# Seven block products for eight in more of the two channel products of an attention and mixer kernel

## The chip, the cores and the metric

The kernel runs on one core of a Trainium2 chip. The metric is the device time of one execution in microseconds (us). The core's engines work side by side, each through its own list of instructions: PE (TensorE, matmuls; PEld is its weight loads), DVE (VectorE), ACT (ScalarE), POOL (GpSimd, which here only issues the input loads) and SP (SyncE, which issues transposing transfers and stores). An instruction that waits holds up everything behind it on its engine.

## The reference

Shapes: q, k, v are (8 batches, 12 heads, 448 tokens, 64); the two token weights are 448x256 and 256x448, the two channel weights 768x1536 and 1536x768.

```python
scores = scale * np.matmul(q, k.transpose(0, 1, 3, 2))
attn = np.maximum(scores, 0.0) ** 2 / S
x = np.matmul(attn, v)                            # heads side by side: (8, 448, 768)
xt = x.transpose(0, 2, 1)
h = np.maximum(xt @ w_tok1, 0.0) @ w_tok2
u = x + h.transpose(0, 2, 1)
h2 = np.maximum(u @ w_ch1, 0.0) @ w_ch2
return u + h2
```

Attention, then a product over the tokens (the token mixer), then two products over the channels: u times w_ch1 is the first channel product, the ReLU of it times w_ch2 the second.

## The kernel before

All work is cut into named operations (class Op), and a long string, ORDER, lists all of them: every engine walks its own operations in the order of that string, and an operation waits only for those that it depends on. A name in ORDER carries after its colon either the engine (A for ACT, D for DVE) or the PSUM banks that it takes (0 to 7).

Attention runs in 24 groups s of four heads, three groups to a batch. POOL loads k, q and v of a group (ldk, ldq, ldv, two each) into four buffers per kind; a load waits until the group four earlier has let its buffer go. Groups 0 to 9 transpose k and q on PE (T, copies cp); from group 10 on DVE copies them into another layout (ik, iq, L435) and SP issues transposing transfers (xk, xq, L439). For each of seven chunks of keys there are the scores (S, L457: four matmuls on quadrants of the array, with two PSUM banks), their ReLU into bf16 (r, L291 on ACT or L293 on DVE), the square on DVE (q, L467) and the value product (V, L484), which adds up over the chunks in two banks. NSQ = 13 buffers hold squared chunks. The result is evicted to xT (xe, L494 and L496), transposed to x_sb (from group 6 on by a transfer that SP issues, xd, L507), and the token product follows: t1 (L528), its ReLU rt, t2 (L537) and the sum u (L541 on DVE), which is written to uT. A second transposing transfer, ub (L549), brings u into the layout of the output, u_sb.

Two batches make a pair p, with 2 x 448 tokens in seven tiles of 128. The first channel product of a batch (C1, L562) takes for each of 12 blocks of 128 hidden rows six matmuls of 448 columns; c1e (L291, ACT) writes its ReLU to r2. The second (C2, L624) takes for a tile of 128 tokens and each half of the 768 output columns twelve matmuls of 384 columns; c2e (L631, DVE) adds u_sb and writes out_sb, which SP stores (st, L608). uT, u_sb and r2 exist twice, one for the even and one for the odd pairs.

FAST1 and FAST2 name the pairs in which a product is done with seven block products instead of eight: both matrices are cut into 2x2 blocks, sums of blocks are formed ahead of the products, and the products are added to each other afterwards. The weight sums (w1, w2), the sums of u (tu) and of r2 (h) are formed on DVE (L639). In the first product of pair 3 (fast1) the two batches are the two column blocks, so the matmuls have 448 columns (M1, L683); a product that two blocks of the result need is copied out of its bank by ACT (snap, L690), the bank goes on adding the next product, and DVE joins the copy with another bank into r2 (L695); a ReLU on r2 in place follows (z1). In the second product of pairs 2 and 3 (fast2) tiles t and t + 4 are the two row blocks (M2, L748), and DVE adds the products to out_sb one after the other (L759, L761). The middle tile of a pair goes through the plain C2. The block sums of the weights and the copies lie in the arena, the buffers of attention, and in other buffers that are free once attention has ended.

## Time and profile before

| | |
|---|---|
| median of 3 runs | 354.97 us (354.52 to 355.62) |
| the profiled execution | 355.15 us |
| its span, first to last instruction | 353.4 us |
| granted TensorE clock, mean | 0.995 |
| busy ACT, POOL | 193.8 us (55%), 91.8 us (26%) |
| read from and written to HBM | 43.38 MB, 11.01 MB |

The page of the profile gives the busy time of each engine, strips of the span in 40 equal slices (a digit is the busy share in tenths, 9 is 90% or more), the chain of work that ended last, and groups of instructions by line, operation and shape (count, busy us, mean ns of one, then the engine's idle time ahead of them and what ended it). The ends of matmuls are modelled, so two matmuls in a row overlap in the records; the distance from start to start tells what one occupies. DVE's records overlap in the same way: a sum of 448 columns lasts 0.62 us in the records and the next one starts earlier.

### The profile page before, as it was taken

What the parts mean: (1) busy time and instruction counts of PE and PEld (TensorE: products, weight loads), DVE (VectorE), ACT (ScalarE), POOL (GpSimd) and SP (SyncE); (2) the same over time, 40 slices, a digit from 0 to 9 for tenths busy, and PEclk for the clock granted to TensorE, in tenths of its full rate; (3) what the DMA queues carried; (4) which work ended last, traced back from release to release, by engine and by line L of the source; (5) the groups of instructions that cost most, each with busy time, mean ns of one, the idle gap of its engine ahead of it and who ended that gap; (6) DMA issues with size and microseconds to landing.
All of it is one profiled execution on the core that took longest, in us unless ns stands there. A gap on an engine that the chain in (4) does not pass through costs nothing.

```text
span 353.4 us, 8749 instructions
## 1 busy us (share of the span) xinstructions
PE 343.5 (97%) x3489; PEld 191.3 (54%) x3489; DVE 294.8 (83%) x580; ACT 193.8 (55%) x395; POOL 91.8 (26%) x157
## 2 busy tenths in 40 slices
PE   7799999999999999999999999999999999999994
PEld 3456455665555555555555555555545555565663
DVE  3999996878875897989988788978999999995661
ACT  3999996644752666727656565456496165400000
POOL 9886214331460423334403250410000000000000
PEclk9899999999999999999999999999999999999999
DMA  8999999999999989998999899979145220034426
GB/s 151 183 171 163 165 183 206 162 122 155 194 192 130 172 184 156 206 197 158 179 199 140 169 138 176 186 176 184 39 60 92 46 59 2 0 85 141 110 65 183
DMA packets 98297, 50.16 MB, mean 142 GB/s; under 512 B 71440, under 2 KB 94800, under 8 KB 98256
## 3 DMA queue, kind: packets, MB, share of 16 engines
q1 hardware_dynamic: 72880, 27.93, 47.7%
q0 software_dynamic: 25136, 21.47, 46.4%
q8 instruction: 27, 0.44, 0.5%
q10 hardware_dynamic: 240, 0.20, 0.2%
q14 instruction: 14, 0.11, 0.1%
HBM read 43.38 MB, written 11.01 MB: 154 GB/s over the span
## 4 chain that ended last, share of the span: by engine, by line
PE 91%; DVE 5%; DMA 1%; ACT 0%; issue 0%; SPq 0%
PE m_ps L562 24%; PE m_ps L624 18%; PE m_ps L748 12%; PE sc_ps L457 10%; PE acc_ps L484 9%; PE m_ps L683 7%; PE t_ps L528 6%; PE h_ps L537 5%; DVE arena L467 2%; DMA arena<-in_q_dram 1%; PE kqT_ps L414 1%; DVE uT_sb L541 1%; DVE arena L639 1%; PE x_ps L519 1%; DVE arena L293 1%; DVE arena L299 1%
## 5 line engine op out<-in xcount | busy, mean ns | idle before, releaser
L291 ACT ACTIVATE arena<-sc_ps 128x448 bf16<-128x448 f32 x234 | 112.0, 573 | 28.8 <-PE sc_ps L457 27.6
L467 DVE TENSOR_TENSOR arena<-arena 128x896 bf16<-128x896 bf16 x168 | 97.0, 618 | 0.5
L562 PE MATMUL m_ps<-uT_sb,wc 128*128 128x448 bf16 x432 | 89.5, 353 | 0.6 <-DVE uT_sb L541 0.6
L293 DVE TENSOR_SCALAR arena<-sc_ps 128x448 bf16<-128x448 f32 x102 | 59.5, 617 | 9.7 <-PE sc_ps L457 9.6
L624 PE MATMUL m_ps<-wc,r_sb 128*128 128x384 bf16 (+2 forms) x396 | 66.6, 322 | 0.0
L562 PEld LDWEIGHTS <-wc 128*128 128x128 bf16 x432 | 40.2, 98 | 43.1 <-issue 9.2
L291 ACT ACTIVATE r_sb<-m_ps 128x448 bf16<-128x448 f32 x72 | 39.7, 553 | 42.4 <-PE m_ps L562 41.9
L313 POOL DMA_DIRECT2D arena<-in_v_dram x48 | 29.3, 620 | 118.3 <-PE sc_ps L457 75.2
L457 PE MATMUL sc_ps<-arena 64*64 64x448 bf16 x672 | 54.4, 361 | 0.7 <-DVE arena L299 0.2
L624 PEld LDWEIGHTS <-r_sb 128*128 128x128 bf16 x396 | 37.7, 98 | 26.3 <-issue 2.6
L484 PE MATMUL acc_ps<-arena 64*64 64x448 bf16 x672 | 49.2, 358 | 1.8 <-DVE arena L467 1.8
L541 DVE TENSOR_TENSOR uT_sb<-h_ps,xT 128x448 bf16<-128x448 f32 x48 | 28.6, 618 | 5.9 <-PE h_ps L537 5.8
L313 POOL DMA_DIRECT2D arena<-in_k_dram x48 | 29.6, 629 | 14.8 <-DMA wc<-in_moe_w_ch_dram 6.5
L457 PEld LDWEIGHTS <-arena 64*64 64x64 bf16 x672 | 20.5, 107 | 20.7 <-issue 12.6
L313 POOL DMA_DIRECT2D arena<-in_q_dram x46 | 28.7, 639 | 9.3 <-PE sc_ps L457 4.7
L484 PEld LDWEIGHTS <-arena 64*64 64x64 bf16 x672 | 20.8, 108 | 15.5 <-issue 6.8
L631 DVE TENSOR_TENSOR out_sb<-m_ps,u_sb 128x384 f32<-128x384 f32 (+2 forms) x31 | 16.8, 543 | 14.3 <-PE m_ps L624 14.1
L291 ACT ACTIVATE r_sb<-t_ps 128x512 bf16<-128x512 f32 (+1 forms) x26 | 15.0, 585 | 20.1 <-PE t_ps L528 20.0
L528 PE MATMUL t_ps<-x_sb,wt 128*128 128x256 bf16 (+1 forms) x216 | 25.4, 261 | 0.0
L537 PE MATMUL h_ps<-wt,r_sb 128*128 128x448 bf16 x96 | 23.8, 354 | 0.0
L528 PEld LDWEIGHTS <-wt 128*128 128x128 bf16 x216 | 19.0, 98 | 7.1 <-issue 1.8
L435 DVE COPY arena<-arena 128x896 bf16<-128x896 bf16 x28 | 16.9, 612 | 4.3 <-DMA arena<-in_q_dram 2.9
(67 smaller groups left out, 300.1 us busy)
## 6 DMA issues: line engine op xcount, KB each, us to landing
out_dram<-out_sb SPq DMA_DIRECT2D x46, 192.0 KB, 3.9
arena<-in_k_dram POOLq DMA_DIRECT2D x48, 112.0 KB, 6.0
arena<-in_v_dram POOLq DMA_DIRECT2D x48, 112.0 KB, 5.3
arena<-in_q_dram POOLq DMA_DIRECT2D x46, 112.0 KB, 7.4
wc<-in_moe_w_ch_dram POOLq DMA_DIRECT2D x6, 768.0 KB, 18.5
out_dram<-xT SPq DMA_DIRECT2D x8, 192.0 KB, 2.8
u_sb<-uT_sb SPq DMA_TRANSPOSE x48, 5.0
arena<-in_q_dram SPq DMA_DIRECT2D x2, 224.0 KB, 3.9
```

The source lines that it names most:

```text
L291: nc.scalar.activation(out, ps, AF.Relu)
L293: nc.vector.tensor_scalar(out=out, in0=ps, scalar1=0.0, scalar2=None, op0=ALU.max)
L313: nc.gpsimd.dma_start(out=raws[t][s % NR][64 * half:64 * (half + 1)], in_=src[b, h0:h0 + 2].rearrange('e (p c) d -> p e (c d)', c=KC))
L457: nc.tensor.matmul(o.ps[e][64 * half:64 * (half + 1), :S], lhsT=lhsT, rhs=rhs, start=True, stop=True, skip_group_check=True)
L467: sq_ops[s, c] = [add(Op(f'q{s}.{c}', 'DVE', lambda o: nc.vector.tensor_tensor(out=buf, in0=buf, in1=buf, op=ALU.mult), ev))]
L484: nc.tensor.matmul(o.ps[half][64 * e:64 * (e + 1), :S], lhsT=r[rows, e, c * D:(c + 1) * D], rhs=sq[rows, e, :], start=c == 0, stop=c == KC ...
L528: nc.tensor.matmul(o.ps[:, j, :], lhsT=wt1[:, c, j * 128:(j + 1) * 128], rhs=x_sb[:, p0:p1, c, :], start=c == 0, stop=c == 3)
L537: nc.tensor.matmul(o.ps[:, :S], lhsT=r1[:, j, a * 128:(a + 1) * 128], rhs=wt2[:, j, :], start=j == 0, stop=j == JC - 1)
L541: nc.vector.tensor_tensor(out=uTs[bb % 2][:, 2 * i + a, off:off + S].rearrange('n (c p) -> n c p', c=KC), in0=t2.ps[:, :S].rearrange('n (p ...
L562: nc.tensor.matmul(ps[:, :S], lhsT=wc1[:, g, e * 128:(e + 1) * 128], rhs=uT[:, g, off:off + S], start=g == 0, stop=g == CC - 1)
L624: nc.tensor.matmul(o.ps[:, :size], lhsT=r2[:, e, t * 128:(t + 1) * 128], rhs=wc2[:, e, cols], start=e == 0, stop=e == EC - 1)
L748: nc.tensor.matmul(o.ps[:, :HN], lhsT=lhs[:, e], rhs=rhs[:, e], start=e == 0 and not on, stop=e == EC // 2 - 1, skip_group_check=True)
```

## The change

The first product is done with seven products in every batch from 2 on (FIRST1), each batch by itself: its 448 tokens are cut into two halves of 224, and a product does two blocks of hidden rows (e, e + 1) in the two halves of one PSUM bank, each with three matmuls of 224 columns. m1, m6, m7 and m4 add up in one bank, m5 and m3 in another. Snapshots are kept as fp32 in rows of r2 that are written later. The second product is done with seven products for three pairs of tiles in all four pairs of batches; PAIRS names them. The tile that is left (ALONE) goes through C2, which now multiplies its upper half with the sum of both halves of r2, since one block of wc2 has been replaced in place by a difference.

r2 and u_sb exist once for pairs 0 to 2 (pair 3 takes the arena), uT has room for three batches, which neighbouring pairs share, the weight sums have a buffer of their own, there are 12 buffers for squared chunks instead of 13 and four output buffers instead of three (two more in the arena at the end). ORDER is replaced from group 5 of attention on; the entries ahead of that are the same. By count of its entries: 27 C1 and 9 C2 (before 75 and 33), 126 M1 and 84 M2 (42 and 42), 54 snapshots (18), 54 joins (24), 84 sums into out_sb behind M2 (48), 52 sums of r2 (48), 24 sums of u (4), 36 z1 and 18 y1 (12 z1); of the score copies r, 284 on ACT and 52 on DVE (234 and 102).

```diff
 NSIDE = 2
 SPLIT = 1
 FUSED = set()
-FAST1, FAST2 = ({3}, {2, 3})
-TILES = [*range(14), 14, 18, 15, 19, 16, 20, 17, 21, 25, 22, 26, 23, 27, 24]
+FIRST1 = 2
+PAIRS = {0: [(0, 1), (3, 4), (5, 6)], 1: [(4, 5), (0, 1), (2, 3)]}
+PAIRS[2], PAIRS[3] = PAIRS[0], [(5, 6), (0, 1), (2, 3)]
+ALONE = [2, 6, 2, 4]
+TILES = [7 * p + t for p, order in enumerate(((0, 1, 2, 3, 4, 5, 6), (4, 5, 6, 0, 1, 2, 3), (0, 1, 2, 3, 4, 5, 6), (5, 6, 0, 1, 2, 3, 4))) for t in order]
+
 
 class Op:
 
...
-r15.2.1:D V14.5 V14.6 r15.6.0:A S16.4:14 r15.6.1:D ldv18.0 C2.1.0.1:7 xe14.0:A xe14.1:D r16.4.0:A ldv18.1
-q15.1:D r16.4.1:A xd14 ldk19.0 q15.2:D ldk19.1 q15.5:D S16.3:26 S16.5:53 ldq19.0 S16.2:01 r16.3.0:A c2e1.0.1:D
...
+r15.0.1:A V14.4 u13.1:D V14.5 V14.6 ldq19.0 S16.0:65 tu3.1:D M1.3.0.1:1 r16.0.1:A q15.0:D ldv16.0 r16.0.0:A
+M2.1.4.4 q15.3:D ldq20.1 s1.3.0.1:A xe14.1:A M1.3.0.3 d2.1.4.21:D xe14.0:A tu3.3:D S15.5:75 S15.6:63 S16.1:42
+r15.5.0:A q16.0:D xq18 M1.3.0.6 r16.1.1:A r15.5.1:D r15.6.1:A M1.3.0.2:7 q15.2:D r16.1.0:A C2.1.6.1:2 xq17
+d1.3.0.11:D q15.1:D s1.3.0.2:A q15.5:D r15.6.0:A xd14 d1.3.0.12:D M1.3.0.7 q15.4:D S16.4:53 V15.0:47 xk18
...
-    NR, NQ, NSQ, NX, NO = (4, 3, 13, 3, 3)
+    NR, NQ, NSQ, NX, NO = (4, 3, 12, 3, 4)
...
-    uTs = [sbuf.tile([128, CC, 2 * S], BF16, name=f'uT_sb{i}') for i in range(2)]
-    u_sbs = [sbuf.tile([128, CC, NT, 128], BF16, name=f'u_sb{i}') for i in range(2)]
-    r2s = [sbuf.tile([128, EC, 2 * S], BF16, name=f'r2_sb{i}') for i in range(2)]
+    uT_all = sbuf.tile([128, CC, 3 * S], BF16, name='uT')
+    uT2 = [uT_all[:, :, p % 2 * S:p % 2 * S + 2 * S] for p in range(B // 2)]
+    u_sb = sbuf.tile([128, CC, NT, 128], BF16, name='u_sb')
+    r2 = sbuf.tile([128, EC, 2 * S], BF16, name='r2')
...
+    u_sbs = [u_sb] * 3 + [arena[:, late['u'][0]:late['u'][1]].rearrange('p (g t n) -> p g t n', g=CC, t=NT)]
+    r2s = [r2] * 3 + [piece(late['r2'][0], EC * 2 * S, EC)]
...
+    def side(b):
+
+        return (b % 2 ^ b // 2 % 2) * S
+
+    def whole(p, b):
+
+        return range(3) if p % 2 == 0 and b == 0 else range(3, NT) if p % 2 == 0 else range(4, NT) if b == 0 else range(4)
+
+    def uslot(p, t):
+        return t if p % 2 == 0 else (t + 3) % NT
...
+    def tokens(p, t):
+
+        got = []
+        for b in (2 * p, 2 * p + 1):
+            if side(b) < (t + 1) * 128 and t * 128 < side(b) + S:
+                for e in range(EC):
+                    got += c1e[b, e]
+        return got
+
+    def u_part(p, t, g0, g1):
+        b = [b for b in range(2) if t in whole(p, b)][0]
+        return (u_sbs[p][:, g0:g1, uslot(p, t), :], [ub[2 * p + b, g] for g in range(g0, g1)])
+
+    def add2(name, dst, x, y, op, deps, **kw):
+        return add(Op(name, 'DVE', lambda o: nc.vector.tensor_tensor(out=dst, in0=x, in1=y, op=op), deps, **kw))
+
+    def sum_set(p):
+        k = sum_n[p == 3] % (1 if p < 3 else 3)
+        sum_n[p == 3] += 1
+        return (rsum[k], sum_free[k])
...
+        rows = tokens(bb, t)
+        (both, _, _), free = sum_set(bb)
+        h = add2(f'h{bb}.{t}.s', both, r2[:, :EC // 2, at], r2[:, EC // 2:, at], ALU.add, rows + free[0])
+        free[0] = []
...
+                    x = both[:, e - EC // 2] if high and e >= EC // 2 else r2[:, e, at]
+                    nc.tensor.matmul(o.ps[:, :size], lhsT=x, rhs=wc2[:, e, cols], start=e == 0, stop=e == EC - 1)
...
             if k == 2:
                 x = one(0, dst[0], w12, w11, ALU.subtract, [])
+                one(3, w12, w12, w22, ALU.subtract, x)
                 y = one(1, dst[1], w22, dst[0], ALU.subtract, x)
-                one(2, dst[2], w22, w12, ALU.subtract, [])
-                one(3, dst[3], dst[1], w21, ALU.subtract, y)
+                one(2, dst[2], w21, dst[1], ALU.subtract, y)
             else:
                 x = one(0, dst[0], w21, w22, ALU.add, [])
...
+    def fast1(b):
+        p = b // 2
+        r2, off = (r2s[p], side(b))
+        uT = uT2[p][:, :, off:off + S]
+        first = b % 2 == 0 and p % 2 == 0
+        half = [slice(HB, S), slice(0, HB)] if first else [slice(0, HB), slice(HB, S)]
+        u11, u12, u21, u22 = (uT[:, g:g + 3, c] for g in (0, 3) for c in half)
+        parts = [[ue[s, a] for a in range(2)] for s in range(GS * b, GS * (b + 1))]
+        low, high = (parts[0] + parts[1][:1], parts[1][1:] + parts[2])
+        every = low + high
+        tu, free = ([u12, *tu_own], [] if b == FIRST1 else reads1[b - 1]) if b < 7 else (tu_late, users(*late['tu']))
+        t3_ = add2(f'tu{b}.2', tu[2], u22, u12, ALU.subtract, every + free)
+        t1_ = add2(f'tu{b}.0', tu[0], u12, u11, ALU.subtract, low + [t3_] + [ub[b, g] for g in range(3)] if b < 7 else low + free)
+        t2_ = add2(f'tu{b}.1', tu[1], u22, tu[0], ALU.subtract, [t1_] + high + free + (snap_free[0] if b < 7 else []))
+        t4_ = add2(f'tu{b}.3', tu[3], u21, tu[1], ALU.subtract, [t2_] + high + free)
+        free2 = [o for t in range(NT) if p and off < (t + 1) * 128 and t * 128 < off + S for o in reads2[p - 1, t]] if p < 3 else users(*late['r2'])
+        reads1[b] = []
+        got, spare = ({}, {})
+        for e in range(0, EC // 2, 2):
+
+            def product(name, lhs, rhs, deps, on=None):
+                o = Op(f'M1.{b}.{e}.{name}', 'PE', None, deps, banks=0 if on else 1, holder=on)
+
+                def emit(o, e=e):
+                    for j in range(2):
+                        for g in range(3):
+                            nc.tensor.matmul(o.ps[:, j * HB:(j + 1) * HB], lhsT=lhs[:, g, (e + j) * 128:(e + j + 1) * 128], rhs=rhs[:, g], start=j == g == 0 and not on, stop=g == 2, skip_group_check=True)
+                reads1[b].append(o)
+                got[e, name] = add(o)
+                return o
+
+            def block(hi, c):
+                return r2[:, hi * 6 + e:hi * 6 + e + 2, off + half[c].start:off + half[c].stop]
+
+            def two(u):
+                return u.ps[:, :S].rearrange('p (j n) -> p j n', j=2)
+
+            def snap(name, dst, u, deps):
+                return add(Op(f's1.{b}.{e}.{name}', 'ACT', lambda o: nc.scalar.activation(dst, two(u), AF.Copy), [u, *deps], reads=[u]))
+
+            def join(name, dst, x, u, deps):
+                o = add(Op(f'd1.{b}.{e}.{name}', 'DVE', lambda o: nc.vector.tensor_tensor(out=dst, in0=x, in1=two(u), op=ALU.add), [u, *deps], reads=[u]))
+                got[e, 'd' + name] = o
+                return o
+
+            def fp32(row):
+                return r2[:, row:row + 2, off:off + S].bitcast(FP32)
+            A = lambda i, h: wc1[:, 3 * i:3 * i + 3, h * DC // 2:(h + 1) * DC // 2]
+            inside = fp32(6 + e)
+            before1 = free2 + ([got[2, 'd22']] if e == 4 else [])
+            m1 = product('1', A(0, 0), u11, every + ([got[e - 2, '5']] if e else []))
+            m2 = product('2', A(1, 0), u21, every)
+            a1 = snap('1', inside, m1, before1)
+            c11 = join('11', block(0, 0), inside, m2, [a1] + ([got[0, 'd22']] if e == 4 else []))
+            m6 = product('6', ws1[1], tu[1], [t2_, a1] + ws_ops[1, 1], m1)
+            a2 = snap('2', inside, m6, [c11])
+            m5 = product('5', ws1[0], tu[0], [t1_] + ws_ops[1, 0])
+            if e == 4:
+                k = 0 if b < 6 else 1 + b % 2
+                x, deps = (snaps[k], [got[i, '6'] for i in (0, 2, 4)] if b < 6 else snap_free[k])
+            else:
+                x, deps = (fp32(4 if e == 0 else 10), free2)
+            a5 = snap('5', x, m5, deps)
+            m3 = product('3', ws1[2], u22, every + [a5] + ws_ops[1, 3], m5)
+            c12 = join('12', block(0, 1), inside, m3, [a2])
+            za = add(Op(f'z1.{b}.{e}.a', 'DVE', lambda o, e=e: relu(o, r2[:, e:e + 2, off:off + S], r2[:, e:e + 2, off:off + S]), [c11, c12]))
+            m7 = product('7', A(0, 1), tu[2], [t3_, a2] + ws_ops[1, 2], m1)
+            c22 = join('22', block(1, 1), x, m7, [a5, c12])
+            if e == 4:
+                snap_free[k] = [c22]
+            zc = add(Op(f'z1.{b}.{e}.c', 'DVE', lambda o, d=block(1, 1): relu(o, d, d), [c22]))
+            m4 = product('4', A(1, 1), tu[3], [t4_, c22], m1)
+            y = add(Op(f'y1.{b}.{e}', 'ACT', lambda o, d=block(1, 0), m4=m4: relu(o, d, two(m4)), [m4, c12], reads=[m4]))
+            for j in range(2):
+                c1e[b, e + j] = [za]
+                c1e[b, 6 + e + j] = [zc, y]
+
...
+    def fast2(p, t, q):
+        r2 = r2s[p]
+        (s1, s2, s4), free = sum_set(p)
+        out1, parts, store1 = stores(p, t)
...
+        x = add2(f'h{p}.{t}.0', s1, h21, h22, ALU.add, co + free[0])
+        y = add2(f'h{p}.{t}.1', s2, s1, h11, ALU.subtract, [x] + ce + free[1])
+        w = add2(f'h{p}.{t}.2', h21, h21, h11, ALU.subtract, [x] + ce)
+        z = add2(f'h{p}.{t}.3', s4, h12, s2, ALU.subtract, [y] + free[2])
+        w2 = list(wc2_ops.values())
+        m2 = product('2', r2[:, e_hi, te], wc2[:, e_hi, c_lo], ce + w2)
+        m1 = product('1', r2[:, e_lo, te], wc2[:, e_lo, c_lo], ce + w2)
+        f11 = take('11a', t, c_lo, m2, [], True)
+        g11 = take('11b', t, c_lo, m1, [f11], False)
+        m6 = product('6', s2, ws2[1], [y, g11] + ws_ops[2, 1], m1)
+        f12 = take('12a', t, c_hi, m6, [], True)
+        m5 = product('5', s1, ws2[0], [x] + ws_ops[2, 0])
+        f22 = take('22a', q, c_hi, m5, [], True)
+        m3 = product('3', s4, wc2[:, e_hi, c_hi], [z, f22] + w2, m5)
+        g12 = take('12b', t, c_hi, m3, [f12], False)
+        m7 = product('7', r2[:, e_lo, to], wc2[:, e_lo, c_hi], [w, f12] + ws_ops[2, 3], m1)
+        g22 = take('22b', q, c_hi, m7, [f22], False)
+        m4 = product('4', r2[:, e_hi, to], ws2[2], co + [g22] + ws_ops[2, 2], m1)
+        g21 = take('21', q, c_lo, m4, [], True)
+        free[:] = [[m5, y], [m6, z], [m3]]
+        for n, s_, ends in ((t, store1, [g11, g12]), (q, store2, [g21, g22])):
+            s_(f'{p * NT + n}', slice(0, DM), ends)
...
+            if b == FIRST1:
...
+            if b < FIRST1:
+                for e in range(EC):
                     channel1(b, e, b == 0 and e < PARTIAL)
+            else:
+                fast1(b)
+            if p < 3:
+                done = [t for t in range(NT) if t in whole(p, b % 2)]
+                todo = [x for x in PAIRS[p] if x[0] in done]
+                first, then = (todo, [ALONE[p]] if ALONE[p] in done else [])
+            else:
+                first, then = ([x for x in PAIRS[p] if x[0] in whole(p, b % 2)], [ALONE[p]] if b % 2 else [])
+            for x, y in first:
+                fast2(p, x, y)
+            for x in then:
```

546 lines of the change are left out of this document (249 added, 297 removed).

## The prediction

> **What bounds the kernel now.** I read the page first: the busy sums, then the strips of 40 slices.
>
> ```profile
> span 353.4 us, 8749 instructions
> ...
> PE 343.5 (97%) x3489; PEld 191.3 (54%) x3489; DVE 294.8 (83%) x580; ACT 193.8 (55%) x395; POOL 91.8 (26%) x157
> ...
> PE   7799999999999999999999999999999999999994
> ...
> DVE  3999996878875897989988788978999999995661
> ```
>
> TensorE (PE) is busy for 97% of the span. VectorE (DVE) is second with 83%, and its strip shows nines beside the sevens: averages hide where it binds. So I asked for the busy time in five stretches (columns: stretch, length, busy PE, PEld, DVE, ACT, POOL, clock, DMA share, GB/s).
>
> ```profile
> 34.70:118.50 83.80, 83.80 (x1038) 46.80 (x1036) 67.96 (x126) 54.22 (x111) 26.83 (x45) 1.00 1.36 170
> 118.50:251.50 133.00, 133.00 (x1222) 72.89 (x1221) 114.33 (x212) 79.43 (x167) 36.20 (x61) 1.00 1.12 168
> 251.50:301.40 49.90, 49.30 (x367) 25.57 (x365) 49.90 (x110) 27.98 (x53) 0.00 (x0) 1.00 0.30 53
> 301.40:332.50 31.10, 31.10 (x191) 18.48 (x189) 24.86 (x58) 3.80 (x4) 0.00 (x0) 1.00 0.33 88
> 332.50:353.40 20.90, 15.84 (x110) 10.05 (x107) 9.75 (x19) 0.00 (x0) 0.00 (x0) 0.99 0.42 115
> ```
>
> PE has no idle time from 34.7 to 251.5 us, with DVE at 81 to 86%. From 251.5 to 301.4 DVE is busy for 49.90 of 49.90 us: that stretch holds the weight sums, the sums for the last first product and the end of attention. From 301.4 on PE alone binds. A modelled end can make a waiting PE look busy, so the chain of waits is the test:
>
> ```profile
> 279.52 21.10 PE m_ps L683 x111
> ...
> 307.36 37.05 PE m_ps L748 x228
> ```
>
> Both products that already use seven blocks for eight (L683 and L748) run as unbroken PE work: 21.10 us for 111 matmuls is 0.190 us each at 448 columns, 37.05 us for 228 is 0.1625 us each at 384 columns. PE is at its streaming rate where no attention runs, although L683 hands a bank to ACT or DVE between products. Less streaming is therefore worth nearly its whole price, as long as DVE keeps up.
>
> **The change on PE.** What one matmul occupies is read from start to start in the order of time (start, length, what, count):
>
> ```profile
> 27.34 0.61 PE L528 MATMUL t_ps<-x_sb,wt 128*128 128x128 bf16 x8
> 27.79 0.39 PE L519 MATMUL x_ps<-ident,xT 128*128 128x128 bf16 x4
> ...
> 99.67 1.87 PE L562 MATMUL m_ps<-uT_sb,wc 128*128 128x448 bf16 x9
> 101.37 1.04 PE L528 MATMUL t_ps<-x_sb,wt 128*128 128x256 bf16 x8
> 102.24 0.92 PE L537 MATMUL h_ps<-wt,r_sb 128*128 128x448 bf16 x4
> ```
>
> 128 columns: (27.79 - 27.34)/8 = 0.056 us. 448 columns: (101.37 - 99.67)/9 = 0.189. 256 columns: (102.24 - 101.37)/8 = 0.109. The new narrow matmuls have 224 columns and no row of their own; on the line between 128 and 256 they cost 0.056 + 96/128 x 0.053 = 0.0957 us. The ends are half a 448 (0.0945) and a full 256 (0.109). I take 0.0957, since 128 to 448 lie on one line.
>
> ```profile
> L562 PE MATMUL m_ps<-uT_sb,wc 128*128 128x448 bf16 x432 | 89.5, 353 | 0.6 <-DVE uT_sb L541 0.6
> L624 PE MATMUL m_ps<-wc,r_sb 128*128 128x384 bf16 x372 | 64.6, 327 | 0.0
> ...
> L528 PEld LDWEIGHTS <-wt 128*128 128x128 bf16 x216 | 19.0, 98 | 7.1 <-issue 1.8 <-DMA arena<-in_q_dram 0.4 <-DMA x_sb<-xT 0.4
> ```
>
> First product: now 432 matmuls of 448 (L562, batches 0 to 5) and 126 at L683 (3 each in 42 products): 558 x 0.189 = 105.5 us. After: 12 x 6 = 72 for each of batches 0 and 1, 144 x 0.189 = 27.2; for each of six batches 3 row pairs x 7 products x 6 = 126 narrow ones, 756 x 0.0957 = 72.3. Sum 99.5: **-6.0 us**, all of it from batches 2 to 5 (6 and 7 go from 23.8 to 24.1). At the ends -6.9 and +4.0.
>
> Second product: now 372 of 384 columns, 12 more in the split last tile, and 252 at L748, 636 in all. After: twelve pairs of tiles x 42 and four single tiles x 24 = 600. 36 x 0.1625 = **-5.9 us**. PE together: **-11.9 us**.
>
> The row of weight loads at L528 speaks to the narrow price: one load for each matmul, 98 ns long each, and still the eight matmuls of 128 columns above start 56 ns apart, so the loads overlap. The Trainium skill ("TensorE: Matmul & The Clock Gate", section "LDWEIGHTS (loading the stationary operand)") states columns/1.2 ns for a load, 107 ns here; if loads followed each other at that price, 756 x (0.107 - 0.0957) = 8.5 us would come back, an estimate from that page. The 56 ns disagree with it as a floor.
>
> **The change on DVE.** Again from start to start:
>
> ```profile
> 166.74 2.75 DVE L467 TENSOR_TENSOR arena<-arena 128x896 bf16<-128x896 bf16 x5
> 169.41 0.55 DVE L631 TENSOR_TENSOR out_sb<-m_ps,u_sb 128x384 f32<-128x384 f32 x1
> ...
> 270.99 1.43 DVE L639 TENSOR_TENSOR arena<-r_sb 128x384 bf16<-128x384 bf16 x5
> 272.34 0.35 DVE L639 TENSOR_TENSOR arena<-arena,r_sb 128x384 bf16<-128x384 bf16 x1
> 272.61 1.49 DVE L639 TENSOR_TENSOR arena<-wc 128x768 bf16<-128x768 bf16 x3
> 274.01 1.49 DVE L639 TENSOR_TENSOR arena<-arena,wc 128x768 bf16<-128x768 bf16 x3
> ...
> 288.34 0.70 DVE L293 TENSOR_SCALAR r_sb<-r_sb 128x896 bf16<-128x896 bf16 x2
> 288.94 0.62 DVE L695 TENSOR_TENSOR r_sb<-x_sb,m_ps 128x448 bf16<-128x448 f32 x1
> ...
> 293.52 0.62 DVE L695 TENSOR_TENSOR r_sb<-r_sb,m_ps 128x448 bf16<-128x448 f32 x1
> 294.05 0.63 DVE L639 TENSOR_TENSOR arena<-r_sb,arena 128x384 bf16<-128x384 bf16 x2
> ...
> 302.87 0.56 DVE L761 TENSOR_TENSOR out_sb<-out_sb,m_ps 128x384 f32<-128x384 f32 x1
> 303.33 0.64 DVE L639 TENSOR_TENSOR arena<-arena,r_sb 128x384 bf16<-128x384 bf16 x2
> ```
>
> Square or PSUM copy of 448 columns (x5): (169.41 - 166.74)/5 = 0.534 us. bf16 sum of 384: 0.27; of 768: (274.01 - 272.61)/3 = 0.467. In-place ReLU of 896: 0.30. Join of a snapshot with a bank: 0.53. Output sum of 384: 0.46.
>
> Counts are from the two written orders. Added: joins 24 to 54, +30 x 0.53 = 15.9. Output sums 81 to 93, 12 x 0.47 = 5.6. Sums of hidden rows, from 48 of 384 elements (12.9) to 52 of 768 (24.3), +11.4. Input sums, from 4 of 1344 (3.1, extrapolated) to 24 of 672 (0.42 by the line, 10.1), +7.0. ReLUs, from 5 of 896 to 18 of 896 and 18 of 448 (between 0 and 0.30, taken 0.19), +7.4. Four ReLUs of y1, five of c1e and two rt that move from ACT, +6. Removed: score copies on DVE 102 to 52, -26.7, and attention evictions 24 to 16, -4.3. Sum **+22 us**: DVE's own work rises from 287 to about 310 us, just above PE's 305. ACT goes from 175 to 191 and has room. The twenty weight sums cost what they did, 11 us, but leave the stretch at 250 to 282 where DVE bound and go into batches 0 and 1.
>
> DVE work costs time only where it exceeds PE's in the same piece of the order. I cut each order into ten stretches of equal PE work, priced every entry as above (S and V at 0.187 for four quadrants together, about one pass of 448) and took the largest engine in each:
>
> before 43.3, 32.0, 31.1, 31.8, 31.6, 31.8, 32.4, 33.5, 31.8, 31.2: 330.4, of which PE 316.8;
> after 41.2, 32.2, 31.7, 32.2, 31.5, 31.7, 30.4, 31.1, 30.2, 30.3: 322.5, of which PE 304.9.
>
> DVE is the larger one in stretches 2 to 6 of after and in the eighth. The surplus over PE goes from 13.6 to 17.6: **+4.0 us** of the gain is given back. With 40 stretches it is +6.8, with 60 +1.8; these are the ends. The 23 us between 330.4 and the span (the first load, the last store, a few tenths at each handover) I leave as they are.
>
> **Transfers.** Counts stay (48 ub, 18 xd, 28 crossings, 60 stores, the same loads). SP and POOL are walked in order, so what counts is the cover: the PE work listed between a transfer and its user. Loads of k gain cover (7.9 to 36 us of DVE work to the crossing copy, before 3.7 to 13); those of v range wider (5.3 to 59 us of PE work, before 9 to 47). One u_sb and one r2 in place of two make ub wait for the outputs of the pair before; the shortest covers are 5.2 to 6.3 us for four of 48, free at the end. The xd transposes (xT to x_sb, before each token product t1) lose cover: in the loaded phase eight have 4.1 to 6.3 us, where before none had under 9.0. While t1 waits, PE's whole queue waits behind it. Now:
>
> ```profile
>   PEld L528: 0.4, 1
> ```
>
> PE's token product waited once. Landing of xd, min/median/max, first in 70 to 235 us, then in 235 to 285 us, where no loads run:
>
> ```profile
> DMA to landing us min/median/max: 4.8/7.8/13.1
> ```
>
> ```profile
> DMA to landing us min/median/max: 3.1/3.6/4.4
> ```
>
> All in time is 0. All eight late at the loaded median is 8 x 7.8 - 1.1 x 42.8 us of summed cover (1.1 is span over priced PE work) = +15.3. The order decides between them: before, a V that frees a v buffer is followed by six loads right ahead of nearly every xd; after, seven of the eight short ones (groups 6, 8, 12, 13, 14, 16, 19) have no load released in the 3 us ahead of them, only up to four behind. They should land near 3.6. Group 7 has seven loads around it. I take **+1.0**.
>
> **Tail.** The last DVE sum now ends at 348.67, 4.7 us before the span does, ahead of a store of 32 KB.
>
> ```profile
> 348.38 0.29 DVE L631 TENSOR_TENSOR out_sb<-m_ps,u_sb 128x128 f32<-128x128 f32 x1 [0.24 <-PE m_ps L624]
> ```
>
> ```profile
> DMA to landing us min/median/max: 1.8/2.8/4.1
> ```
>
> (Landing of the stores after 340 us.) After, two stores of 192 KB follow the last sum on one queue: about 1.0 more to land (2.8 for 1.8) and one more issue: **+1.5**, between 0 and 3.
>
> **Sum.** -11.9 + 4.0 + 1.0 + 1.5 = -5.4 us: span 353.4 - 5.4 = 348.0. The profiled execution took 355.15, 1.75 around the span: 349.7. It stood 0.2 above the median of the runs (354.97): **349.5 us**. Its own range, from the ends of the DVE and tail terms, is 346 to 353.
>
> **Rivals.**
> PE alone binds. DVE's surplus is absorbed as in the 251.5 to 301.4 stretch, where DVE ran without a gap, so stretches even out: -11.9 + 1.5 = -10.4, 344.6 us. For it: PE loses nothing after 301.4. Against: there DVE had twenty weight sums that nobody waited for at once.
> Late transposes, the slower side. Place: t1 of groups 6 to 19. Price: up to 15.3, and with five of eight late 9.6, which gives 349.5 - 1.0 + 9.6 = 358.1. It decides from 6.4 us in all, 0.8 for each of the eight. For it: the 7.8; against: the 3.6 without loads.
> Handover chains. Each row pair passes one bank through m1, snapshot, m6, snapshot and join, m7, m4; with DVE full, each hop waits in its queue. 18 pairs x 0.3 us = 5.4: 354.9, no change. For it: DVE's nines; against: the unbroken 21.10 us at L683.
> Narrow products gain nothing: 0.109 each, as 256 columns, +10.1: 359.6. Against: 56 ns at 128 columns. (The 107 ns that the Trainium skill's page above states for a weight load would end in the same place, 358.0, by its estimate.) That the products aren't cut at all is excluded by the counts in the order (126 M1, 84 M2).
>
> **How the numbers follow.** Forecast 0.52, PE alone 0.17, late transposes 0.18, chains 0.10, narrow 0.03. A measurement of this kernel tells about 0.3% (1.1 us) from no change. Faster takes nearly all of the first two and a third of the chains: 0.71; same 0.08 (chains, a mild case of late transposes); slower 0.21. The range reaches down past PE alone with less lost at the tail, 343, and up to the late transposes' 358.
>
> **What would show it.** 756 matmuls of 224 columns 0.096 us apart (not 0.107); 504 + 96 of the second product; PE busy near 331 us; DVE busy 94 to 96% from 35 to 270 us; waits of the token product for x_sb under 2 us in total; weight sums between 45 and 90 us; no DVE-bound stretch at the end. It is wrong if PE waits for x_sb or for joins by more than 6 us, or if the span is set by DVE gaps rather than PE's.

## The result, and the profile after

The changed kernel took 352.83 us (median of 20 runs, 350.96 to 356.98), the kernel before 355.29 us beside it (20 runs, 354.08 to 360.06): a ratio of 0.9934, 95% interval 0.9909 to 0.9959. It is faster by 0.7%, some 2.3 us, where 5.4 us were forecast. A second set gave 353.5 us (11 runs) and 0.9952 (0.9919 to 0.9984). The ratios leave out the longest runs as disturbed; where this document gives means, they hold all runs, because what lengthens them is part of the question, and without the longest ones too the mean granted clock is 0.9953 before and 0.9904 after.

The page of the changed kernel's first profiled execution (it took 356.81 us, the next to longest of the 20):

```profile
span 355.0 us, 9385 instructions
...
PE 338.9 (95%) x3795; PEld 218.7 (62%) x3795; DVE 316.1 (89%) x630; ACT 209.2 (59%) x441; POOL 92.0 (26%) x157
...
PE   7799999999999799999969999999999999999993
...
PEclk9999999999999989999996999999999999999999
```

and of another execution of the same kernel, in experiment e1:

```profile
span 350.2 us, 9385 instructions
...
PE 335.4 (96%) x3795; PEld 217.2 (62%) x3795; DVE 316.0 (90%) x630; ACT 209.5 (60%) x441; POOL 91.8 (26%) x157
...
PE   8799999999998979979999999999999999999993
...
PEclk9999999999999999999999999999999999999998
```

One program, 4.8 us apart. PE now shows sevens and sixes in the middle, where before had only nines, and in the longer execution the granted clock dips in the slices right behind them (an 8 and a 6). So I read the spans of e1's execution for the work and the waits, and the first one for what the clock adds. The kernel before had 53 runs beside the experiments; with the changed kernel's 31 the means are 355.86 and 353.60 us, 2.3 us apart.

The busy time of e1's execution in the stretches that the prediction showed for before (columns as there; the last row runs from 35 to 270 us):

```profile
34.70:118.50 83.80, 82.60 (x1023) 44.40 (x1020) 79.96 (x151) 56.97 (x117) 25.66 (x43) 1.00 1.11 163
118.50:251.50 133.00, 128.98 (x1368) 85.42 (x1367) 126.10 (x254) 99.63 (x215) 37.36 (x63) 1.00 1.08 164
251.50:301.40 49.90, 49.90 (x495) 38.08 (x494) 47.58 (x96) 17.95 (x36) 0.00 (x0) 1.00 0.35 66
301.40:332.50 31.10, 31.10 (x266) 24.98 (x264) 24.35 (x53) 5.84 (x12) 0.00 (x0) 1.00 0.50 99
332.50:350.20 17.70, 12.13 (x75) 7.08 (x73) 9.29 (x19) 0.00 (x0) 0.00 (x0) 0.93 0.49 123
35.00:270.00 235.00, 229.78 (x2573) 144.27 (x2567) 223.71 (x440) 163.46 (x345) 62.88 (x106) 1.00 1.05 159
```

From 34.7 to 251.5 us PE used to have no idle time at all; now 5.2 us are missing (83.80 - 82.60 + 133.00 - 128.98). DVE is at 95% of that time. The stretch from 251.5 us, where DVE used to be busy without a gap, has PE without a gap instead.

Where the time went shows when both spans are cut into the prediction's ten stretches of equal PE work, whose larger engine it priced at 330.4 us in all before and at 322.5 after. The span takes 23.0 us more than that sum before, 27.7 in e1's execution: if PE and DVE together brought the -7.9 of the sum, +4.7 stand behind it. The 4.7 lie in the third to the fifth stretch. First before, then e1:

```profile
86.40:118.50 32.10, 32.10 (x272) 17.66 (x271) 24.20 (x45) 18.48 (x38) 11.26 (x19) 1.00 1.38 172
118.50:151.80 33.30, 33.30 (x312) 17.78 (x311) 28.86 (x55) 21.15 (x45) 12.47 (x22) 1.00 1.19 179
151.80:184.70 32.90, 32.90 (x313) 18.16 (x315) 29.67 (x56) 19.14 (x41) 8.31 (x15) 1.00 1.19 178
```

```profile
83.10:117.40 34.30, 33.23 (x310) 17.14 (x299) 32.16 (x63) 23.85 (x52) 5.37 (x10) 1.00 1.16 167
117.40:152.40 35.00, 32.93 (x356) 22.57 (x354) 32.51 (x66) 25.48 (x56) 13.06 (x22) 1.00 1.13 158
152.40:186.90 34.50, 32.55 (x343) 20.36 (x341) 31.78 (x63) 25.77 (x56) 14.50 (x25) 1.00 1.16 180
```

They took 98.3 us before and 103.8 after. The priced work of the larger engine went from 94.5 to 95.4 us (31.1, 31.8, 31.6 and 31.7, 32.2, 31.5), so time beyond it went from 3.8 to 8.4 us: +4.6. The other seven stretches together moved by 0.1 us. (Before's profile has a stretch of halved clock at 15 to 18 us and e1's has none: in the same order of work the first row of ten matmuls of 448 columns starts at 39.27 us before and at 38.64 in e1, so the 0.1 holds to some 0.6.) In these three stretches DVE is the larger engine by price, 95.4 us; it was busy for 96.5 and idle for 7.4, of which 5.8 are the waits for u_sb below.

The waits of e1's execution (who, for what; us in all, times, longest), PE's first, then DVE's:

```profile
PE t_ps L574 <- DMA x_sb<-xT: 2.3, 2, 2.0
...
PE m_ps L833 <- DVE out_sb L846: 1.5, 1, 1.5
```

```profile
DVE uT L672 <- DMA u_sb<-uT: 3.8, 2, 2.1
...
DVE out_sb L846 <- DMA u_sb<-uT: 2.0, 1, 2.0
```

The first is the token product t1 (L574) waiting for its transpose xd, of which the prediction had spoken. The second is PE waiting for DVE, and the DVE rows say why: DVE waits for u_sb, the transposing copies ub. Neither DVE row exists before. `DVE uT L672` is tu{b}.0, the first sum of a batch's input columns. It is written in place over a block of uT that the copies ub still have to read.

The first profile shows such a chain, and what follows it. In the order of time (start, length, what, and in brackets the idle time before it):

```profile
123.51 0.51 DVE L672 TENSOR_TENSOR uT<-uT 128x672 bf16<-128x672 bf16 x1 [3.13 <-DMA u_sb<-uT]
123.93 0.55 DVE L846 TENSOR_TENSOR out_sb<-u_sb,m_ps 128x384 f32<-128x384 bf16 x1
...
124.53 1.85 PE L833 MATMUL m_ps<-wc,r 128*128 128x384 bf16 x6 [2.06 <-DVE out_sb L846]
```

DVE stands at tu2.0 for 3.13 us; behind it in its queue is the sum that empties a bank (L846); the second product waits 2.06 us for that bank. Then its six matmuls take 1.85 us, where six of 384 columns took 1.14 elsewhere. The clock says why (the same view in stretches cut where the granted clock changes, then the same around a wait of 3.65 us of t1.14 for x_sb that ended at 187.0):

```profile
121.40:124.80 3.40, 1.34 (x16) 0.70 (x14) 1.29 (x3) 1.91 (x4) 3.28 (x7) 1.00 0.95 137
124.80:128.20 3.40, 3.40 (x30) 1.50 (x31) 3.40 (x8) 1.06 (x3) 3.40 (x7) 0.50 1.26 199
...
182.00:186.20 4.20, 1.39 (x15) 1.14 (x12) 1.41 (x3) 2.37 (x6) 3.42 (x6) 1.00 1.54 146
186.20:193.10 6.90, 6.06 (x33) 3.63 (x34) 3.50 (x8) 2.29 (x5) 0.00 (x0) 0.51 1.18 204
```

After a stretch in which PE is busy for about a third, it runs at half its clock for 3.4 or 6.8 us: up to half of that, 1.7 and 3.4 us, is lost on top of the wait. The halved stretch begins 2.3 us after the wait did in the first case (124.53 - 2.06 = 122.47, then 124.8), 2.8 us after in the second. Over the 20 runs the time follows the mean clock: 351.48 us at 0.995, 356.98 us at 0.981.

### The profile page after: what moved, and what is told of

Read it like the earlier page. It is cut to its first block, busy times and chain, and to the rows that moved or that the text cites. A ratio compares the mean times of both kernels' runs of the same rounds, so it can differ in the third digit from the quotient of the medians.

```text
span 355.0 us, 9385 instructions
## 1 busy us (share of the span) xinstructions
PE 338.9 (95%) x3795; PEld 218.7 (62%) x3795; DVE 316.1 (89%) x630; ACT 209.2 (59%) x441; POOL 92.0 (26%) x157
## 4 chain that ended last, share of the span: by engine, by line
PE 82%; DMA 7%; DVE 7%; ACT 1%; issue 1%; POOL 0%; SPq 0%; DVEq 0%; POOLq 0%; ACTq 0%
PE m_ps L764 21%; PE m_ps L833 20%; PE sc_ps L503 9%; PE acc_ps L530 8%; PE m_ps L609 8%; PE t_ps L574 6%; PE h_ps L583 5%; PE m_ps L697 4%; DMA x_sb<-xT 2%; DVE arena L513 2%; DMA u_sb<-uT 2%; DMA arena<-in_k_dram 1%; DMA out_dram<-out_sb 1%; PE kqT_ps L460 1%; ACT arena L337 1%
## 5 line engine op out<-in xcount | busy, mean ns | idle before, releaser
L337 ACT ACTIVATE arena<-sc_ps 128x448 bf16<-128x448 f32 x284 | 137.1, 568 | 34.8 <-PE sc_ps L503 30.5
L764 PEld LDWEIGHTS <-wc 128*128 128x128 bf16 x432 | 40.8, 98 | 6.7 <-issue 3.9
L764 PEld LDWEIGHTS <-ws 128*128 128x128 bf16 x324 | 31.1, 100 | 4.9 <-issue 3.0
L339 DVE TENSOR_SCALAR arena<-sc_ps 128x448 bf16<-128x448 f32 x52 | 31.4, 620 | 1.7 <-PE sc_ps L503 1.6
L833 PE MATMUL m_ps<-wc,r 128*128 128x384 bf16 x162 | 30.9, 332 | 2.1 <-DVE out_sb L846 2.1
L833 PEld LDWEIGHTS <-r 128*128 128x128 bf16 x216 | 20.6, 98 | 17.4 <-issue 5.2
L609 PE MATMUL m_ps<-uT,wc 128*128 128x448 bf16 x144 | 30.0, 353 | 0.0
L574 PE MATMUL t_ps<-x_sb,wt 128*128 128x256 bf16 (+1 forms) x216 | 26.2, 266 | 3.6 <-DMA x_sb<-xT 3.6
L587 DVE TENSOR_TENSOR uT<-h_ps,xT 128x448 bf16<-128x448 f32 x48 | 29.1, 622 | 0.5 <-PE h_ps L583 0.4
L777 ACT ACTIVATE arena<-m_ps 128x448 f32<-128x448 f32 x18 | 9.5, 545 | 32.7 <-PE m_ps L764 23.3
L777 ACT ACTIVATE r<-m_ps 128x448 f32<-128x448 f32 x32 | 17.5, 554 | 16.0 <-PE m_ps L764 10.7
L764 PE MATMUL m_ps<-uT,wc 128*128 128x224 bf16 x216 | 25.7, 259 | 0.0
L574 PEld LDWEIGHTS <-wt 128*128 128x128 bf16 x216 | 19.4, 99 | 9.4 <-DMA x_sb<-xT 3.9
```

The lines of the kernel that those rows point to most:

```text
L337: nc.scalar.activation(out, ps, AF.Relu)
L339: nc.vector.tensor_scalar(out=out, in0=ps, scalar1=0.0, scalar2=None, op0=ALU.max)
L574: nc.tensor.matmul(o.ps[:, j, :], lhsT=wt1[:, c, j * 128:(j + 1) * 128], rhs=x_sb[:, p0:p1, c, :], start=c == 0, stop=c == 3)
L587: nc.vector.tensor_tensor(out=uT2[bb][:, 2 * i + a, off:off + S].rearrange('n (c p) -> n c p', c=KC), in0=t2.ps[:, :S].rearrange('n (p c) ...
L609: nc.tensor.matmul(ps[:, :S], lhsT=wc1[:, g, e * 128:(e + 1) * 128], rhs=uT[:, g, off:off + S], start=g == 0, stop=g == CC - 1)
L764: nc.tensor.matmul(o.ps[:, j * HB:(j + 1) * HB], lhsT=lhs[:, g, (e + j) * 128:(e + j + 1) * 128], rhs=rhs[:, g], start=j == g == 0 and not ...
```

## The experiments

Two main theories. **A**: the gain was given back at a few waits for transfers (t1 for xd, tu2.0 and the output sums for ub), each followed by more loss through the clock. **B**: DVE's surplus over PE costs more than the 4.0 us priced. **C**, in some of the expectations: the clock falls by itself, or by a disturbance of the chip, and not after waits. Runs of one kind are put together in this table. "Clock" is the mean granted clock over the span; "by the clock" is span x (1 - clock), what full speed would have saved if PE worked all of the slow time, so an upper bound (e1's profiled execution is halved only from 347.5 us on, when PE has no work left, and still has 1.05 us in this column); "rest" is the time without it. All are means.

| kernel | runs | time us | clock | by the clock | rest |
|---|---|---|---|---|---|
| before | 53 | 355.86 | 0.9953 | 1.68 | 354.18 |
| after (with e1) | 31 | 353.60 | 0.9895 | 3.68 | 349.92 |
| e2: xd14 earlier | 12 | 355.83 | 0.9868 | 4.67 | 351.16 |
| e3 and e10: tu2.0 later | 12 | 352.45 | 0.9949 | 1.79 | 350.66 |
| e4: both | 8 | 352.89 | 0.9925 | 2.64 | 350.25 |
| e5: e3 without ReLUs | 4 | 352.12 | 0.9892 | 3.78 | 348.34 |
| e8 and e11: more cover | 19 | 352.28 | 0.9923 | 2.70 | 349.58 |
| e6: before, xd14 late | 4 | 364.37 | 0.9862 | 4.99 | 359.39 |
| e9: before, xd14 half as late | 4 | 364.00 | 0.9842 | 5.70 | 358.30 |
| e7: e6 with PE kept busy | 4 | 364.19 | 0.9970 | 1.09 | 363.10 |

**e1, the changed kernel again.** No edit.

> The changed kernel once more, for a profile and a ratio beside the variants. Theory A (two transfers come late and PE pays for each twice, once by waiting and once by a halved clock afterwards): the gain over the kernel before is about 2.5 us, ratio 0.993, mean granted clock 0.988 to 0.993 where the kernel before has 0.995, and the waits show PE held for x_sb in front of the token product of group 14 (around 183 us) and DVE held by a transfer out of uT (around 120 us). Theory B (VectorE's surplus work is the loss): no such waits, clock 0.995, DVE above 96% from 35 to 270 us. Theory C (the clock falls by itself, from more power): clock falls at places without a PE wait.

353.5 us (11 runs), ratio 0.9952 (0.9919 to 0.9984). Its profile is the one read above. Against the first profile the waits differ in place and length (the longest for x_sb is 2.0 us here, 3.65 there): which transfer comes late changes from execution to execution.

**e2, one transpose earlier; e3, one sum later; e4, both.** In the written order:

```
e2   d2.1.4.21:D xe14.0:A  + xd14  tu3.3:D
     ...
     r15.6.0:A  - xd14  d1.3.0.12:D
e3   ldv11.0 d2.0.3.12b:D M2.0.5.3  - tu2.0:D  ldq17.0
     ...
     r11.6.1:A d2.0.3.22b:D  + tu2.0:D  V10.5
```

> Only the transfer xd14 is listed earlier on SP, right behind the eviction xe14.0 and so ahead of the crossing transfers xq18 and xq17, which wait for the scores of group 15. Theory A: the transfer is issued about 3 us earlier, PE's wait of 3.7 us in front of t1.14 goes, the clock stays up there, and the time falls by 2 to 5 us against e1 (ratio to the kernel before 0.980 to 0.988). Theory B: no change beyond 0.3%. A rival within A (the landing is slow because of the loads around it, not because of SP's queue): it is issued earlier but still lands at the same time, and nothing changes.

> Only the sum tu2.0, which overwrites part of uT and so waits for the transfer ub2.0 out of it, is listed nine DVE operations later (about 4.5 us). Theory A: DVE's wait of 3.1 us around 120 us goes, with it PE's wait of 2 us behind it, and the time falls by 1 to 3 us against e1. Theory B: no change beyond 0.3%.

> Both moves. Theory A: the gains add up, 3 to 7 us against e1, span 345 to 348 us, clock 0.994 or more, ratio to the kernel before 0.975 to 0.984. Theory B: as e1. Theory C: the clock stays at 0.990 and the time at e1's.

e2 alone gains nothing where 2 to 5 us were expected: median 356.58 us (12 runs), ratio 0.9931 (0.9887 to 0.9975). In its profile t1.14 no longer waits, but the u_sb wait and one for a store are there, and PE waits longer than ever for DVE:

```profile
PE m_ps L833 <- DVE out_sb L846: 6.0, 2, 4.0
...
DVE uT L672 <- DMA u_sb<-uT: 4.6, 1, 4.6
...
DVE out_sb L846 <- DMA out_dram<-out_sb: 2.9, 1, 2.9
```

e3 took 351.06 us (6 runs), ratio 0.985 (0.9811 to 0.989), with a profile of 348.6 us: DVE's wait at L672 for u_sb is gone, 1.3 us for x_sb, 1.7 for u_sb at an output sum and 2.7 for a store remain. e4 gave 352.31 us (8 runs), ratio 0.9869 (0.9822 to 0.9916), and none of these waits in its profile of 349.1 us, which was halved in its clock twice before 20 us; its gain on e1 is 1.2 us by the medians and not the 3 to 7 expected, so the two moves don't add up. These four kernels ran in the same rounds: moving tu2.0 lowers the mean by 2.9 us both without and with e2's move (354.27 to 351.33, 355.83 to 352.89; standard errors 1.1 and 1.3), and e2's move raises it by 1.6 both times, within the noise. So the wait at tu2.0 looks like one cause, and e2's place isn't shown to be one.

**e10, e3 once more.**

> e3_tu2_late a second time. Theory A: again 350 to 352 us, mean clock 0.993 or over. If its six runs were luck, 352 to 353.5 us as the changed kernel, and a mean clock near 0.989.

353.95 us (6 runs, 348.79 to 357.05), ratio 0.9882 (0.9824 to 0.9941), above the 350 to 352 that A expected: with it, the mean of the twelve is 352.45 us, and about half of e3's advantage over the changed kernel (351.33 to 353.60) is gone. Its profile (span 352.9) shows another transfer late, a store of 192 KB from a tile out_sb, with eight loads of POOL issued around it:

```profile
208.95 0.55 DVE L846 TENSOR_TENSOR out_sb<-u_sb,m_ps 128x384 f32<-128x384 bf16 x1 [4.07 <-DMA out_dram<-out_sb]
...
209.56 1.76 PE L833 MATMUL m_ps<-wc,sums 128*128 128x384 bf16 x5 [3.68 <-DVE out_sb L846]
```

```profile
190.00:205.80 15.80, 15.80 (x176) 9.85 (x169) 14.40 (x29) 12.28 (x27) 4.68 (x9) 1.00 1.05 188
205.80:208.20 2.40, 0.07 (x1) 0.00 (x0) 0.00 (x0) 0.00 (x0) 0.66 (x2) 1.00 1.78 85
208.20:215.00 6.80, 5.45 (x25) 2.08 (x25) 3.93 (x8) 0.48 (x2) 1.78 (x3) 0.50 1.40 121
```

For 2.4 us hardly an engine but POOL works; then the clock is halved for 6.8 us. It is the same chain with another transfer at its head.

**e5, less work for DVE.** e3's kernel without the 36 ReLUs in place of the first and third kind:

```
-    za = add(Op(..., lambda o, e=e: relu(o, r2[:, e:e + 2, off:off + S], ...), [c11, c12]))
+    za = add(Op(..., lambda o: None, [c11, c12]))
-    zc = add(Op(..., lambda o, d=block(1, 1): relu(o, d, d), [c22]))
+    zc = add(Op(..., lambda o: None, [c22]))
```

> The kernel of e3_tu2_late with the 36 in-place ReLUs of the hidden rows (first and third kind, batches 2 to 7) left out, so those hidden rows are computed without ReLU: 18 of 896 columns at 0.30 us and 18 of 448 at about 0.19 us, 8.8 us of VectorE's work. Theory A (the gain was given back at a few waits for transfers, and the surplus of VectorE's work over TensorE's is the 4 us that the prediction priced): the most it can return is that surplus, so 0 to 4 us below e3_tu2_late, and the waits for x_sb and u_sb stay. Theory B (VectorE's work is what keeps the time up): it returns nearly all of its work, 6 to 9 us below e3_tu2_late, about 343 to 345 us.

352.02 us (4 runs), beside 352.0 (the median of e3's and e10's twelve); DVE was busy for 309.0 us in place of 315.5. Nowhere near 343 to 345 though DVE had 6.5 us less to do: B falls as the main cause. The rest without the clock is 2.3 us lower (348.34 for 350.66), within A's 0 to 4, but on four runs. One execution again waited 2.0 us for x_sb and ran at half its clock from 158.6 to 162.0 us.

**e6, e9, e7, the price of one wait.** The kernel before, where no such wait existed, with the entry of the transpose for group 14 moved down: in e6 to right in front of t1.14, in e9 some 2.2 us of PE work ahead of it, in e7 as e6 with 28 matmuls of 512 columns between (27 of them recorded).

```
     r16.4.1:A  - xd14  ldk19.0
     ...
e9   iq19:D  + xd14  S17.0:76
e6   r17.1.1:A q17.0:D  + xd14  t1.14.0:6
e7   r17.1.1:A q17.0:D  + xd14 fill:6*112  t1.14.0:6
```

> The kernel before with one entry of its order moved: the transpose of x for group 14 is listed right in front of the token product that reads it. Theory A: TensorE waits once for its landing, 3 to 8 us, and then runs at half its clock for one or two stretches of 3.4 us, which costs 1.7 or 3.4 us more: 4 to 11 us above the kernel before, and more than the wait alone by 1.7 us or over. A rival, C (a wait costs its own length and no more, the halved clock in some profiles is a disturbance of the chip): the time rises by the wait alone, and no halved clock follows the wait.

> As e6_before_xd14_late, with 28 idle-filling products of 448 columns or so (about 6 us, their results are read by nobody) on TensorE between the transpose and the token product: TensorE works while the transfer is under way. Theory A: no halved clock follows, so the time is above the kernel before by the filling work alone, about 5 to 6 us, and where the wait of e6 is as long as this, e7 is faster than e6 by 1.7 to 3.4 us. Rival C: e7 costs as much as the longer of filling and wait, never less than e6.

> The kernel before with the transpose of x for group 14 listed seven entries of TensorE's work (some 2.2 us) ahead of the token product that reads it, where e6_before_xd14_late had it right in front. Theory A (a wait of TensorE also costs a halved clock): a wait of 2 to 5 us, a halved clock in some executions and not in others, mean clock of the runs between those of before (0.995 to 0.997) and of e6 (0.986); 3 to 7 us above the kernel before, more in the executions with the lower clock. Rival C (the wait alone): 2 to 5 us above it, the mean clock that of before.

e6: 364.64 us (4 runs), ratio 1.0242 (1.0187 to 1.0296). e9: 363.91 us (4 runs), 1.0236 (1.0196 to 1.0277). e7: 362.72 us (4 runs), 1.0184 (1.012 to 1.0249). In e6 PE waited once, for 7.4 us; the same product in e7 waited 1.12 us behind 6 us of filling:

```profile
192.69 3.01 SPq L507 DMA_TRANSPOSE x_sb<-xT  x1
...
197.85 1.89 PE L528 MATMUL t_ps<-x_sb,wt 128*128 128x256 bf16 x8 [7.40 <-DMA x_sb<-xT]
```

```profile
190.47 6.21 PE L839 MATMUL fill_ps<-warm 128*128 128x512 bf16 x27
...
192.63 3.11 SPq L507 DMA_TRANSPOSE x_sb<-xT  x1
...
197.80 1.05 PE L528 MATMUL t_ps<-x_sb,wt 128*128 128x256 bf16 x8 [1.12 <-DMA x_sb<-xT]
```

The transpose was issued and landed at the same times. The eight matmuls took 1.89 us in e6 and 1.05 in e7. The same stretch, e6 and then e7:

```profile
192.80:203.00 10.20, 5.15 (x18) 2.59 (x19) 0.24 (x1) 1.14 (x2) 0.00 (x0) 0.50 0.53 120
```

```profile
192.80:203.00 10.20, 9.07 (x49) 4.62 (x48) 2.21 (x4) 1.69 (x3) 0.00 (x0) 1.00 0.58 128
```

All four runs of e6 had a clock of 0.982 to 0.991, all four of e7 0.995 to 0.999. So the halved clock follows the wait, and not the late transfer: rival C, that it is a disturbance of the chip, falls for this place. Of e6's rise (364.37 - 355.86 = 8.5 us) at most 3.3 us are by the clock (4.99 - 1.68), the other 5.2 or more the wait. In the profile half of the 10.2 us at half clock lie in the wait itself, where they cost nothing; the other 5.15, in which PE works, cost 2.6. In time e7 isn't clearly below e6: 1.9 us by the medians, within the 1.7 to 3.4 expected, but the intervals overlap, and one of e7's four runs, 369.72 us, lifts its mean (the other three are at 361.59 to 363.40, e6's at 363.40 to 364.80). e9 shows that 2.2 us of cover weren't enough to help: its wait was 5.8 us, the mean clock no higher (0.984 for 0.986) and the rise 8.1 us, all three outside what was expected.

**e8 and e11, more cover.** e8 is e3 with ub1.0 listed right behind ub1.1, t1.12.0 and t1.13.0 some products later, and tu3.0 some ten DVE operations later; e11 adds one load:

```
e8   S9.1:45 ub1.1  + ub1.0  C1.1.10:7
     y1.2.4:A  - t1.12.0:3  xk16  ...  S14.3:54  + t1.12.0:3  st5.64
     V13.6  - tu3.0:D  M2.1.4.2:0  ...  d2.1.4.11b:D  + tu3.0:D  S14.1:70
     ldv16.1  - t1.13.0:1  r15.4.1:A  ...  c2e1.6.0:D  + t1.13.0:1  rt13.0:A
e11  ldv13.0  + ldv10.0  M2.0.3.5:7  ...  q10.0:D  - ldv10.0  M2.0.3.7
```

> The kernel of e3_tu2_late with four more entries moved, each to give a transfer more cover: the copy ub1.0 right behind ub1.1, the token products of groups 12 and 13 some products later, and the sum tu3.0 some ten VectorE operations later. Theory A: what remained in e3_tu2_late of waits for x_sb (1.3 us) and out_sb (1.7 us) goes, 1 to 3 us below e3_tu2_late, ratio to the kernel before 0.975 to 0.985. Theory B: no difference to e3_tu2_late.

> e8_more_cover with one load of v (ldv10.0) moved some 50 entries up POOL's queue, to where its buffer has come free: in e8_more_cover its product waited 1.2 us for it. Theory A: that wait goes, and with it the last one of over 1 us behind the first 30 us: 347.5 to 351 us, 1 us or so below e8_more_cover. Theory B: as e8_more_cover.

e8: 352.24 us (12 runs), ratio 0.9873 (0.9834 to 0.9911). e11: 352.33 us (7 runs), 0.9916 (0.9884 to 0.9947). In both profiles PE no longer waits for x_sb, and DVE no longer for u_sb; in e11 nothing behind 30 us makes PE wait longer than 1.0 us at once (the first two waits here lie ahead of that), and its span is 348.3 us, 0.3 from the forecast's 348.0:

```profile
PE acc_ps L530 <- DVE arena L513: 1.8, 2, 0.9
PE warm_ps L402 <- DVE out_sb L399: 1.2, 1, 1.2
PE sc_ps L503 <- ACT arena L337: 1.0, 1, 1.0
```

Yet the medians aren't below e3's and e10's 352.0, against what A expected: these moves have no gain of their own that the runs show. The move of tu2.0 has one: put together, the 39 runs with it (e3, e4, e8, e10, e11) have a mean of 352.46 us, the 43 without it (the changed kernel, e1, e2) one of 354.22: 1.8 us apart with a standard error of 0.5, and 1.6 of it by the clock.

## Why the prediction was off

**The direction and the price of the matmuls were right.** The narrow products stand 0.097 us apart, 0.0957 were interpolated: six of them from row to row in e1's order of time,

```profile
229.23 0.75 PE L764 MATMUL m_ps<-uT,ws 128*128 128x224 bf16 x6
229.82 0.74 PE L764 MATMUL m_ps<-uT,wc 128*128 128x224 bf16 x6
230.39 0.74 PE L764 MATMUL m_ps<-sums,ws 128*128 128x224 bf16 x6
230.97 0.74 PE L764 MATMUL m_ps<-uT,ws 128*128 128x224 bf16 x6
```

(230.97 - 229.23)/18 = 0.097 us. All 756 are at L764, and 504 + 96 matmuls of the second product at L833 and L697 as counted (L697 has 108 records, because twelve are split in two). The rivals that narrow products gain nothing and that weight loads bind are out.

**The surplus of DVE isn't contradicted.** No run measures the -7.9 us (330.4 to 322.5) of PE and DVE together alone. For it: outside three stretches nothing moved beyond the sum, in those three DVE was busy for 96.5 us where 95.4 were priced, and e5 bounds what DVE could still return at a few us. DVE is busy for 95.2% from 35 to 270 us (223.71 of 235.00), as said. PE's busy time was to be near 331 and was 335.4: a modelled end lets a PE that waits for DVE look busy, which the prediction itself had warned of; busy and idle together are what counts. "PE alone binds" falls: in the three stretches the time stands beyond DVE's price, not below it. The handover chains as priced, 0.3 us for each of 18 row pairs, fall too: outside the three stretches above time moved by 0.1 us in all, the stretches with products L764 on their own included. Two other signs failed: the weight sums ran from 54.6 to 134.2 us in e1 and not to 90, and in the three stretches it is DVE's gaps that set the span.

**The tail** was taken at +1.5 and measured about +0.3: the last DVE sum now ends 5.0 us before the span does, 4.7 before.

```profile
344.66 0.55 DVE L846 TENSOR_TENSOR out_sb<-arena,m_ps 128x384 f32<-128x384 bf16 x1 [0.42 <-PE m_ps L833]
```

**The step that failed is the transfers' +1.0.** With PE and DVE as priced and the tail as measured, the mean over the runs gives -2.3 = -11.9 + 4.0 + 0.3 + T, so T, by difference, is 5.3 us. Not all of that is long waits: in e11's execution, which has none, PE is idle for 3.1 us in short pieces between 35 and 270 us, the span is 5.1 us below before, and T is still 2.5. That execution meets the forecast's span because 1.2 us too much at the tail offset 1.5 too little here. Whether the 2.5 are short waits or a DVE surplus above 4.0 stays open. The prediction put it so: "the shortest covers are 5.2 to 6.3 us for four of 48, free at the end", and for xd "They should land near 3.6". Three things were wrong in it.

First, it counted the waits of ub for the outputs of the pair before, not who waits for ub. Writing tu{b}.0 in place into uT makes a DVE sum wait for three copies that read that block; DVE was at 95%, and what stood behind the sum was the emptying of a bank for PE. 3.8 us of DVE waits in e1, 4.6 in e2, none in e3. A new user that *overwrites* is a new waiter, and it stood in the diff: `[t3_] + [ub[b, g] for g in range(3)]`.

Second, a median landing was set against the cover. The median was nearly right, 4.1 for 3.6 us (the landings of xd from 70 to 285 us, least, median and longest, in e1):

```profile
DMA to landing us min/median/max: 3.0/4.1/7.8
```

but with covers of 4 to 6 us it is the long ones that decide, and which are long changes from execution to execution: 8.6 us for xd14 in the first profile, no wait there in e1. The price has to be worked out over the spread, for all short covers together (eight xd and four ub by the prediction's count, and the stores that free out_sb): in six of the nine profiles with the whole change, e5's included, PE waits for 1 us or more at a time behind one that is late, and not always the same one. That is likely why moving single entries (e2, e8, e11) removed the waits that had been seen and gained little; nine profiles don't show it for the other runs.

Third, a late transfer was priced at its lateness. A wait of some 2 us or more could also halve the clock, in the profiles with the whole change for 3.4 or 6.8 us. Over all runs the loss by the clock went from 1.68 to 3.68 us: up to 2.0 of the 5.3. The other 3.3 or more are waits and what e11 leaves open. e6 and e7 show this for one wait in the kernel before; that each halved stretch between 20 us and PE's last work has its wait in front is read from the profiles (2.06 us before 3.4, 3.65 us before 6.8; 3.7 us before 6.8 in e10, 2.0 before 3.4 in e5, 4.0 before 6.8 and 1.9 before 3.4 in e2).

The Trainium skill ("TensorE: Matmul & The Clock Gate", section "What's actually happening") describes a free-running activity window of 3.4 us, and the section "HAM oscillation — how this bites in real kernels" warns of idle gaps longer than that. The lengths agree (3.4, 6.8, 10.2 us); the threshold does not: 2.06 us of idle time were enough here and 1.94 in e2, while 1.95 us in e1 had no halved clock behind them:

```profile
157.24 1.05 PE L574 MATMUL t_ps<-x_sb,wt 128*128 128x256 bf16 x8 [1.95 <-DMA x_sb<-xT]
```

The late transposes' rival (358.1) had named the right kind of loss, with a price for x_sb alone; the waits were fewer than its five of eight. Its point of decision, 6.4 us, was not reached, but PE's waits for x_sb, 2.3 us in e1 and 3.6 in the first profile, were above the 2 us that the prediction allowed.

**Left open.** A buffer of its own for tu0, which would remove the wait at its root, wasn't tried. The profiles of e4, e5 and e8 have two stretches of halved clock before 20 us, that of before has one; what starts them wasn't looked into, and part of the 2.0 us by the clock may be theirs.

## What to carry to other kernels

When a kernel's two busiest engines are both near full, price a transfer by the spread of its landings and by everything that queues behind its waiter, not by its median. For each buffer that becomes single or is written in place, list who must now wait for whom, on the engines as well as on the queues. A wait of TensorE of some 2 us or more should, by these profiles, be priced at its own length plus 1.7 to 3.4 us for the halved clock that may follow.
